# Attention and two gated FFNs on one core: a new plan for the weight chunks, and a new order of the quarter products

## The chip, the core and the metric

One core of a Trainium2 chip runs the whole program. The metric is device time in microseconds (us). TensorE (PE) multiplies, ScalarE (ACT), VectorE (DVE) and GpSimd (POOL) work on tiles, and SyncE (SP) issues nearly all DMAs. Each engine runs its own instructions in order and waits for the others by semaphores.

## The reference, cut to what matters

```python
scores = where(mask, q @ k.T / sqrt(D), -1e9)     # 4 batches, 8 heads, 576 x 64; heads 0-3 local, 4-7 strided
x = softmax(scores) @ v                            # as 2304 tokens x 512
xn = x / sqrt(mean(x * x) + 1e-6) * rms_g
y = (silu(xn @ w_gate) * (xn @ w_val)) @ w_out     # FFN 1, d_ff 1536
out = (silu(y @ w2_gate) * (y @ w2_val)) @ w2_out  # FFN 2, same sizes
```

All in float32. The kernel writes each operand of the FFNs as a sum of a rounded half (`xh`, `hh`, w[:, 0]) and its residual (`xl`, `hl`, w[:, 1]) and multiplies three of the four pairs.

## The kernel before

**Stages.** First the attention of batch 0; then its other batches are woven into the *early segments* of FFN 1: six segments of tokens (256 to 512 wide) times chunks 0 to 5 (a chunk is 128 of the 1536 hidden columns). From about 406 us on come five *passes* (chunks 6 to 8 and 9 to 11 of FFN 1, then 0 to 3, 4 to 7 and 8 to 11 of FFN 2), each over three *blocks* of 768 tokens.

**A chunk in a block.** Gate and value of a chunk are made from two halves of the 768 tokens by a scheme with seven *quarter products* instead of eight. A product is six matmuls of 128 x 384 (`Chunk.mult`). Products 1, 6, 7 and 4 add up in one PSUM bank (x), products 2, or 5 and 3, in another (y). Between them stand helpers: after 1 a *seed* (ACT copies x to y), after 6 and 7 a *keep* (ACT copies x to SBUF), after 2 a silu, which frees y; 5 opens y again, an `add` on DVE reads it, 3 adds to it, and after 4 and 3 a `join` (product, ACT cast to hh, DVE residual hl) ends the use of x and y. Two pairs of banks take turns, so a chunk's x is the bank of the chunk after next. `lower` multiplies by w_out (six matmuls) for one half of the tokens, `blank` the same for the other half of the block before, from the list `left`.

**Weights.** A chunk's words come as three loads of 0.5 MB into a ring of three buffers `raw` (five in the pool `st`, once the attention has ended), are put together by two ACT and two DVE instructions (`scale`: `raw`, `dh`), combined by four POOL subtractions (`sums`), and split into rounded half (ACT) and residual (DVE). Kind c keeps the result in SBUF; p *parks* it in DRAM (`pk`), r *recalls* it later; d does w_out. The text given to `plan` is the order of these. `weights()` is called at each *point* (one or two per product); it starts the next entry when its `ready` allows, and begins its operations `lag` points later, `pace["op"]` per point. A scheduler then puts each engine's instructions in order; `behind` ties a weight operation behind the last urgent one on its engine.

**Activations.** `load_x` fetches an early segment's input into `xraw`, in the same ring as `raw`. `stage_x` fetches the next block's 768 tokens into `xst`, `sum_x` and `split_q` (POOL, with ACT casts) make the next block's operands during this block.

Lines: `matmul` is L66; the weight operations are L227 and L235 (ACT), L239 and L244 (DVE), L326 (POOL sums), L358 (ACT cast), L362 (DVE residual), L370 and L371 (stores); L865 loads xraw, L892 casts hh in the early segments; in the passes L1210 is the keep, L1216 the seed, L1220 the add, L1224 the silu, L1230, L1234 and L1235 the join, L1314 the eviction, L1165 `sum_x`, L1182 the split.

Of the kernel before, what the change touches and what calls it, by code (L numbers as in the profile page):

```python
# [18 lines left out]
PRIO = 200  # L19
# [6 lines left out]
def attn_ffn_ffn(ctx: ExitStack, tc: tile.TileContext, q, k, v, w1g, w1v, w1o, rms_g, w2g, w2v, w2o, out):  # L26
# [178 lines left out]
    rack = {"pool": dec, "free": 3, "bufs": 3, "dh": 2}  # L205
    racks = [rack]
# [15 lines left out]
    def scale(cell, free=1):  # L222

        def high():
            cell["h"] = cell["bk"]["pool"].tile([128, 512], F32, tag="dh", name="dh", bufs=cell["bk"]["dh"])
            with behind("act"):
                nc.scalar.activation(out=cell["h"], in_=cell["hw"].bitcast(F32), func=AF.Copy, scale=2.0 ** -112)  # L227

        def low():
            cell["r"] = cell["lw"]  # L230
            if spare:
                spare.append(spare.pop(0))
                cell["r"] = pp.tile([128, 512], U32, tag=spare[-1], name="lws")
            with behind("act"):
                nc.scalar.activation(out=cell["r"], in_=cell["lw"], func=AF.Copy, scale=LOW)  # L235

        def sign():
            with behind("dve"):
                nc.vector.scalar_tensor_tensor(out=cell["r"], in0=cell["hw"], scalar=0x80000000, in1=cell["r"], op0=ALU.bitwise_and, op1=ALU.bitwise_or)  # L239

        def join():
            h = cell["h"].bitcast(U32)
            with behind("dve"):
                nc.vector.scalar_tensor_tensor(out=h, in0=h, scalar=3, in1=cell["r"], op0=ALU.logical_shift_left, op1=ALU.bitwise_or)  # L244
            cell["bk"]["free"] += free

        return [low, high, sign, join]
# [9 lines left out]
    def weight_step(m, c, z, park=False):  # L257
# [11 lines left out]
        def second():  # L269
            lo(cell["t"], cell["h"])  # L270
            wt[m, c, z] = cell["t"]
            wdone.add((m, c, z))
# [15 lines left out]
        def save():  # L288
# [4 lines left out]
            cell["bk"]["free"] += 1  # L293
# [3 lines left out]
                    lambda: (park or room[4]) and racks[0]["free"] >= 1, PRIO_W)  # L297
# [3 lines left out]
    def combined_step(m, c, how):  # L301
# [7 lines left out]
        def ready():  # L309
            if racks[0]["free"] < 2:  # L310
                return False
            return how == "park" or len(room[4]) >= n4 and len(room[2]) >= 7 - 2 * n4
# [7 lines left out]
        def sums():  # L320
# [4 lines left out]
            for z, a, b in ((0, b12, b11), (2, b22, b12), (1, b22, t[:, 0]), (3, b21, t[:, 1])):  # L325
                nc.gpsimd.tensor_tensor(out=t[:, z], in0=a, in1=b, op=ALU.subtract)  # L326
# [17 lines left out]
        def op(i, f):  # L344
            def g_():
                f(*parts[i])
                if i == len(parts) - 1 and f is (save if how == "park" else second):
                    g["bk"]["free"] += 1
                    if how == "park":
                        v["bk"]["free"] += 1  # L350
# [661 lines left out]
    plan("p19 p110 c16 d16 c17 c18 d17 d18 r19 d19 r110 d110 p111 p20 r111 d111 p21 r20 d20 r21 d21 p22 p23 r22 d22 r23 d23 "  # L1012
# [40 lines left out]
    def first_x():  # L1053
# [33 lines left out]
        for kk in range(2):  # L1087
            eager.extend((add("s1", "a21", "a22", ALU.add, kk), split(1, "a11", kk), split(4, "a22", kk), split(5, "s1", kk),
                          add("a21", "a11", "a21", ALU.subtract, kk), add("a11", "s1", "a11", ALU.subtract, kk), split(2, "a12", kk),
                          split(7, "a21", kk), add("a12", "a12", "a11", ALU.subtract, kk), split(6, "a11", kk), split(3, "a12", kk)))  # L1090
# [4 lines left out]
    for si, (m, t0, n, c0, c1) in enumerate(segs):  # L1095
# [11 lines left out]
        pace["op"] = 2.0  # L1107
        xs = xs_of.pop(si)
        state["tanh"] = True and att is not None
        for c in range(c0, c1):  # L1110
# [6 lines left out]
            if att and not steps and not active_att():  # L1117
# [6 lines left out]
                racks.insert(0, {"pool": pools["st"][0], "free": 5, "bufs": 5, "dh": 5})  # L1124
# [68 lines left out]
    class Chunk:  # L1193
# [44 lines left out]
        def step(self, i):  # L1238
# [104 lines left out]
    for n, (m, cs, t0) in enumerate(work):  # L1343
# [52 lines left out]
        state["lag"], state["wait"] = 10 if n else 5, 9  # L1396
        for z in (1, 0, 0, 2, 6, 0, 5, 7, 0):
            step(chunks[0], z) if z else blank()
            if z == 5 and nxt:
                cell = stage_x(nxt[0], nxt[2])  # L1400
            if z == 2:
                spare[:] = ya[halves[0].n:]
        for i, c in enumerate(chunks[:-1]):
            c1 = chunks[i + 1]
            step(c1, 1)
            step(c, 4)
            step(c, 3)
            if t0 + 2 * HN == NT:
                used((m, c.c, False))
            step(c1, 2)  # L1410
            if i == 0 and nxt:
                sum_x(cell)
            if i == k - 2:
                pace["op"] = 0.6 if n else 0.8
# [5 lines left out]
            if i == k - 2:  # L1420
                for j in J:
                    halves[0].fetch(j)
            while left:
                blank()
            lower(i, 0)
        c = chunks[-1]
        spare.clear()
        step(c, 4)
        step(c, 3)
        if t0 + 2 * HN == NT:  # L1430
            used((m, c.c, False))
        left = [piece(halves[1], c, g, other_done if g is G[-1] and c is chunks[-1] else None) for g in G for c in chunks]
        lower(k - 2, 1)
        blank()
        blank()
        for j in J:
            halves[1].fetch(j)
        lower(k - 1, 0)
        lower(k - 1, 1)
        blank()  # L1440
# [35 lines left out]
```

## Time and profile before

| | us |
|---|---|
| median of 3 runs (1057.32 to 1061.37) | 1059.54 |
| profiled execution | 1058.73 |
| its span | 1056.9 |
| PE busy | 992.2 (94%) |
| DVE, ACT, POOL busy | 589.0, 575.5, 472.9 |
| mean granted clock of PE | 0.964 |
| DMA | 181.60 MB, 172 GB/s |

PE is the busiest engine. In the page's 40 slices it is below 9 tenths in the first six (the attention), in the sixteenth and the twenty-second. A wait's row names the waiting instruction, the releaser and three numbers: us in total, times, longest. The granted clock is 1.00 at 2.4 GHz and 0.50 at 1.2 GHz.

### The profile page before, as it was taken

The numbers are of one execution on the slowest core, as the hardware profiler recorded it, in microseconds if no ns is written. First come the engines' busy times: TensorE is split into PE (matmuls) and PEld (weight loads), VectorE is DVE, ScalarE is ACT, GpSimd is POOL, SyncE is SP. The second block draws the span as 40 slices with busy tenths as digits, with TensorE's granted clock in tenths as the row PEclk, the third lists the DMA queues.
The fourth block names the chain that finished last, engine by engine and source line by source line (L and its number), as shares of the span: only waits on it lengthen the run. The fifth ranks groups of instructions, "written<-read, shape, count | busy, mean of one in ns | idle before, by whom it ended". The sixth has DMA issues, their size and how long they took to land. (4 is left out here: it accounts for less than half of the span.)

```text
span 1056.9 us, 16819 instructions
## 1 busy us (share of the span) xinstructions
PE 992.2 (94%) x5804; PEld 905.4 (86%) x5804; DVE 589.0 (56%) x1289; ACT 575.5 (54%) x1435; POOL 472.9 (45%) x485
## 2 busy tenths in 40 slices
PE   5758979999999997999987999999999999999998
PEld 4647869878778986999987999999998999899997
DVE  3779546445434186764756666555547665633433
ACT  5878745636633355753663565656547455643431
POOL 3312212203100294675956865837557473745500
PEclk9758989999999998999999999999999999999999
DMA  7576445224105129677687595257862739815021
GB/s 196 157 221 182 146 135 161 66 65 127 40 26 185 53 89 348 203 251 243 209 256 246 201 343 181 92 188 255 285 237 75 254 126 349 269 64 180 30 80 60
DMA packets 153277, 181.60 MB, mean 172 GB/s; under 512 B 44132, under 2 KB 120364, under 8 KB 153192
## 3 DMA queue, kind: packets, MB, share of 16 engines
q1 hardware_dynamic: 153000, 180.25, 52.6%
q8 instruction: 46, 0.75, 0.3%
q14 instruction: 39, 0.32, 0.1%
q0 software_dynamic: 192, 0.28, 0.1%
HBM read 123.60 MB, written 56.89 MB: 171 GB/s over the span
## 5 line engine op out<-in xcount | busy, mean ns | idle before, releaser
L1182 POOL TENSOR_TENSOR xl<-xst,xh 128x384 fp32r<-128x384 f32 x168 | 185.6, 1136 | 70.9 <-PE b_a L66 42.8
L66 PE MATMUL b_y<-xh,w 128*128 128x384 f32 x700 | 188.6, 336 | 4.0 <-ACT t L1210 4.0
L66 PE MATMUL b_g<-xh,w 128*128 128x384 f32 (+2 forms) x496 | 150.8, 352 | 9.7 <-ACT xh L905 7.0
L66 PEld LDWEIGHTS b_y<-xh,w 128*128 128x128 f32 x700 | 127.6, 188 | 7.6 <-ACT t L1210 5.7
L66 PE MATMUL b_a<-xh,w 128*128 128x384 f32 (+2 forms) x460 | 126.3, 338 | 5.6 <-DVE t L1220 5.5
L66 PE MATMUL b_v<-xh,w 128*128 128x384 f32 (+2 forms) x432 | 129.7, 350 | 0.0
L66 PE MATMUL b_y<-hh,w 128*128 128x256 f32 (+2 forms) x432 | 119.1, 347 | 3.7 <-ACT hh L892 3.7
L66 PE MATMUL b_y<-xl,w 128*128 128x384 f32 x350 | 117.4, 335 | 0.0
L66 PEld LDWEIGHTS b_g<-xh,w 128*128 128x128 f32 x496 | 93.3, 196 | 16.4 <-ACT xh L905 7.2
L66 PEld LDWEIGHTS b_a<-xh,w 128*128 128x128 f32 x460 | 83.9, 189 | 9.6 <-DVE t L1220 6.0
L635 POOL TENSOR_TENSOR e<-e,rc 128x384 f32<-128x384 f32 (+3 forms) x40 | 38.3, 961 | 119.6 <-DVE rc L629 84.3
L1181 ACT CAST xh<-xst 128x384 fp32r<-128x384 f32 x168 | 80.2, 522 | 12.5 <-POOL xst L1165 12.4
L66 PEld LDWEIGHTS b_y<-hh,w 128*128 128x128 f32 x432 | 78.3, 191 | 10.1 <-ACT hh L892 4.0
L66 PEld LDWEIGHTS b_v<-xh,w 128*128 128x128 f32 x432 | 79.7, 192 | 6.7 <-issue 0.4
L66 PE MATMUL b_g<-xl,w 128*128 128x384 f32 (+2 forms) x248 | 85.4, 344 | 0.0
L66 PE MATMUL b_a<-xl,w 128*128 128x384 f32 (+2 forms) x230 | 77.6, 337 | 0.0
L66 PE MATMUL b_y<-hl,w 128*128 128x256 f32 (+2 forms) x216 | 73.8, 342 | 2.4 <-DVE hl L893 1.7
L1165 POOL TENSOR_TENSOR s<-xst 128x384 f32<-128x384 f32 x28 | 28.8, 1049 | 104.5 <-DMA xst<-y_d 71.8
L66 PE MATMUL b_v<-xl,w 128*128 128x384 f32 (+2 forms) x216 | 73.5, 340 | 0.0
L66 PEld LDWEIGHTS b_y<-xl,w 128*128 128x128 f32 x350 | 65.7, 188 | 1.8
L66 PE MATMUL b_y<-w,hh 128*128 128x512 f32 x216 | 67.1, 392 | 0.0
L618 ACT ACTIVATE e<-e,nb 128x96 f32<-128x96 f32 (+2 forms) x152 | 56.6, 376 | 19.2 <-DVE nb L609 19.2
(210 smaller groups left out, 2198.3 us busy)
## 6 DMA issues: line engine op xcount, KB each, us to landing
w<-pk SPq DMA_DIRECT2D x39, 512.0 KB
pk<-raw SPq DMA_DIRECT2D x65, 256.0 KB
xst<-y_d SPq DMA_DIRECT2D x18, 768.0 KB
raw<-in_moe_w_gate_dram SPq DMA_DIRECT2D x24, 512.0 KB
raw<-in_moe_w_val_dram SPq DMA_DIRECT2D x24, 512.0 KB
raw<-in_moe_w_out_dram SPq DMA_DIRECT2D x24, 512.0 KB
part<-ob SPq DMA_DIRECT2D x48, 256.0 KB
ob<-part SPq DMA_DIRECT2D x36, 256.0 KB
```

The costliest lines, as they stand in the source:

```text
L66: traced(nc.tensor.matmul(out_, a, b_, start=start, stop=stop, **how))
L618: r = nc.scalar.activation(out=e[:qn, i, :kn], in_=e[:qn, i, :kn], func=AF.Exp, bias=nb[:qn, i:i + 1], scale=-1.0, accum_out=sums[:qn, i:i ...
L635: eng.tensor_tensor(out=e[:qn, :nt, :kn], in0=e[:qn, :nt, :kn], in1=rc[:qn, :nt].unsqueeze(2).to_broadcast([qn, nt, kn]), op=ALU.mult)
L1165: eng.tensor_tensor(out=out_[:, kk], in0=a[:, kk], in1=b[:, kk], op=op)
L1181: nc.scalar.copy(out=xh[:, kk], in_=src[:, kk])
L1182: eng.tensor_tensor(out=xl[:, kk], in0=src[:, kk], in1=xh[:, kk].bitcast(F32), op=ALU.subtract)
```

## The change

- **Plan.** Before, 13 chunks were parked (9, 10, 11 of FFN 1 and ten of FFN 2); now 11: chunk 6 of FFN 1 is parked and recalled, chunk 11 of FFN 1 and chunks 0 and 1 of FFN 2 are kept. A chunk is only parked once the attention has ended (`att is None`).
- **Counts.** A released buffer counts as free 6 points later; a second count (`words`) of buffers limits the first operation of a chunk, and rises 4 to 8 points after the last use.
- **Lags and paces** change (in the passes 12 points from load to first operation, where it was 9), POOL's sums get a higher priority, and product 6's split comes earlier in `first_x`.
- **Order of the products.** A chunk's products 7 and 5 now stand in the next cycle, and 6 before 2; x is staged after the first product of a block; the fetches of partial sums stand earlier.

```diff
-            fit = [st for st in begun if clock[0] - st.at >= st.lag]
+            fit = [st for st in begun if clock[0] - st.at >= st.lag and (not hasattr(st[0], "cell") or words(st[0].cell["bk"]) > 0)]
...
+    def back(bk, n):
+        bk["back"].append((clock[0] + 6, n))
...
+    def spent(bk, n):
+        bk["wback"].append(clock[0] + n)
+        bk["wback"].sort()
...
-            return how == "park" or len(room[4]) >= n4 and len(room[2]) >= 7 - 2 * n4
+            return how == "park" and att is None or how != "park" and len(room[4]) >= n4 and len(room[2]) >= 7 - 2 * n4
...
-            for z, a, b in ((0, b12, b11), (2, b22, b12), (1, b22, t[:, 0]), (3, b21, t[:, 1])):
-                nc.gpsimd.tensor_tensor(out=t[:, z], in0=a, in1=b, op=ALU.subtract)
+            with tc.high_priority(offset=PRIO):
+                for z, a, b in ((0, b12, b11), (2, b22, b12), (1, b22, t[:, 0]), (3, b21, t[:, 1])):
+                    nc.gpsimd.tensor_tensor(out=t[:, z], in0=a, in1=b, op=ALU.subtract)
...
-    plan("p19 p110 c16 d16 c17 c18 d17 d18 r19 d19 r110 d110 p111 p20 r111 d111 p21 r20 d20 r21 d21 p22 p23 r22 d22 r23 d23 "
+    plan("p16 p19 p110 r16 d16 c17 c18 d17 d18 p22 r19 d19 r110 d110 p23 c111 d111 c20 d20 c21 d21 r22 d22 r23 d23 "
...
-        pace["op"] = 2.0
+        pace["op"] = 2.5 if si < NA - 1 else 1.5
+        state["lag"], state["wait"] = (6, 6) if att is None else (3, 4)
...
                 self.mult(self.y, 5, True)
+                self.add(self.vb, self.vb)
             elif i == 7:
                 self.mult(self.x, 7, False)
                 self.vb = self.keep("t3", 2)
-                self.add(self.vb, self.vb)
...
-        state["lag"], state["wait"] = 10 if n else 5, 9
-        for z in (1, 0, 0, 2, 6, 0, 5, 7, 0):
-            step(chunks[0], z) if z else blank()
-            if z == 5 and nxt:
-                cell = stage_x(nxt[0], nxt[2])
...
+        state["lag"], state["wait"] = 10 if n else 8, 12
+        step(chunks[0], 1)
+        blank()
+        if nxt:
+            cell = stage_x(nxt[0], nxt[2])
+        blank()
+        spare[:] = ya[halves[0].n:]
+        step(chunks[0], 6)
+        if len(left) > 2:
+            blank()
+        step(chunks[0], 2)
         for i, c in enumerate(chunks[:-1]):
             c1 = chunks[i + 1]
             step(c1, 1)
+            step(c, 7)
+            step(c, 5)
+            blank()
+            lower(i - 1, 0)
             step(c, 4)
+            if i == k - 3 and nxt:
+                sum_x(cell)
+            step(c1, 6)
+            step(c1, 2)
             step(c, 3)
...
-            step(c1, 2)
-            if i == 0 and nxt:
-                sum_x(cell)
...
-            step(c1, 6)
-            blank()
-            lower(i - 1, 1)
-            step(c1, 5)
-            step(c1, 7)
...
             while left:
                 blank()
-            lower(i, 0)
+            lower(i - 1, 1)
```

SP's queue in the attention, about 85 to 120 us, before: `raw` are weight loads, `pk_9` the parking of chunk 9.

```order
L812 DMA x_d_1_994<-x_410 128x2x320
L218 DMA raw<-in_moe_w_out_dram 128x1024
L218 DMA raw<-in_moe_w_gate_dram 128x4x256
L218 DMA raw<-in_moe_w_val_dram 128x4x256
L218 DMA raw<-in_moe_w_gate_dram 128x4x256
L475 DMA qn_1292<-in_q_dram 108x1x320 x4
L477 DMA qn_1292<-in_q_dram 18x4x128
```

The same place now.

```order
L838 DMA x_d_1_961<-x_378 128x2x320
L237 DMA raw<-in_moe_w_out_dram 128x1024
L891 DMA xraw<-x_d_1_961 128x2x256 x2
L891 DMA xraw<-x_d_1_961 128x2x64 x2
L501 DMA qn_1246<-in_q_dram 108x1x320 x4
L503 DMA qn_1246<-in_q_dram 18x4x128
```

The three loads of chunks 9 and 10 have gone, and the loads of the second segment's input stand in their place.

ACT's queue at the end of the early segments, before: the last `sg` and `hh`, then the first seed of the passes (`b_v<-b_g`).

```order
L884 ACTIVATE sg<-b_a_4484 128x512
L235 ACTIVATE raw<-raw 128x512
L227 ACTIVATE dh<-raw 128x512
L358 CAST w_8_5_4482<-raw 128x512
L892 CAST hh<-sg 128x512
L251 CAST w_7_2_4548<-dh 128x512
L235 ACTIVATE raw<-raw 128x512
L358 CAST w_8_7_4483<-raw 128x512
L227 ACTIVATE dh<-raw 128x512
L251 CAST w_8_2_4574<-dh 128x512
L1216 COPY b_v<-b_g 128x384
```

The same place now; the first two `raw` and `dh` are chunk 8's gate, the second two its value, the third `raw` is w_out of chunk 7.

```order
L910 ACTIVATE sg<-b_a_4476 128x512
L255 ACTIVATE raw<-raw 128x512
L247 ACTIVATE dh<-raw 128x512
L918 CAST hh<-sg 128x512
L255 ACTIVATE raw<-raw 128x512
L247 ACTIVATE dh<-raw 128x512
L384 CAST w_8_1_4547<-dh 128x512
L1243 COPY b_v<-b_g 128x384
L384 CAST w_8_3_4548<-dh 128x256
L255 ACTIVATE raw<-raw 128x512
L76 COPY ob<-b_y_4331 128x512
L76 COPY ob<-b_y_4333 128x512
```

The load that ACT needs between `sg` and `hh` is another one, and chunk 8's work stands nearer to the passes.

ACT's queue in a cycle of a block of the first pass, before; each product leaves one row. `t_5482` and `t_5513` are the keeps of chunk 6's products 6 and 7, `t_5576` and `t_5591` those of chunk 7.

```order
L1210 COPY t_5482<-b_g 128x384
L1210 COPY t_5513<-b_g 128x384
L1216 COPY b_a_5523<-b_a_5516 128x384
L1224 ACTIVATE b_g<-b_g 128x384
L1234 CAST hh<-b_g 128x384
L1224 ACTIVATE t_5563<-b_a_5523 128x384
L1234 CAST hh<-b_v 128x384
L1210 COPY t_5576<-b_a_5516 128x384
L1210 COPY t_5591<-b_a_5516 128x384
L1216 COPY b_v<-b_g 128x384
```

The same cycle now; `t_5490` and `t_5519` are the keeps of chunk 6, `t_5564` and `t_5605` those of chunk 7.

```order
L1237 COPY t_5490<-b_g 128x384
L1251 ACTIVATE t_5499<-b_v 128x384
L1243 COPY b_a_5511<-b_a_5504 128x384
L384 CAST raw<-raw 128x512
L1237 COPY t_5519<-b_g 128x384
L1251 ACTIVATE b_g<-b_g 128x384
L1237 COPY t_5564<-b_a_5504 128x384
L1261 CAST hh<-b_g 128x384
L1251 ACTIVATE t_5572<-b_a_5511 128x384
L1261 CAST hh<-b_v 128x384
L1237 COPY t_5605<-b_a_5504 128x384
L1208 CAST xh<-xst 128x384 x2
```

The keep of product 7 has moved behind the next chunk's seed, and the silu after product 4 (`b_g<-b_g`) stands nearer to that bank's next use.

## Rows read from the trace of the kernel before

**Rows 1.** Busy us (and instructions) by stretch: PE, PEld, DVE, ACT, POOL; clock, DMA.

```profile
325.00:406.60 81.60, 81.60 (x464) 72.06 (x463) 42.77 (x59) 36.60 (x72) 37.79 (x33) 1.00 0.41 133
406.60:419.20 12.60, 7.25 (x19) 5.35 (x18) 9.36 (x13) 7.73 (x14) 5.32 (x6) 0.59 0.94 344
419.20:1056.90 637.70, 623.29 (x3339) 590.73 (x3338) 356.40 (x568) 334.60 (x726) 362.38 (x356) 0.99 0.58 196
```

**Rows 2.** What PE waited for: us in total, times, longest.

```profile
PE b_g L66 <- ACT xh L905: 7.0, 1, 7.0
PE b_a L66 <- DVE t L1220: 5.5, 1, 5.5
PE b_y L66 <- ACT t L1210: 4.0, 4, 2.9
PE b_y L66 <- ACT hh L892: 3.7, 1, 3.7
...
PE b_a L69 <- issue: 2.3, 1, 2.3
PE b_y L66 <- DVE hl L893: 1.7, 1, 1.7
```

**Rows 3.** Stretches right after PE's waits, columns as in rows 1.

```profile
122.10:125.40 3.30, 3.27 (x19) 2.81 (x20) 1.77 (x12) 2.30 (x11) 0.66 (x1) 0.51 0.53 180
138.90:142.60 3.70, 3.63 (x16) 3.43 (x17) 1.88 (x4) 1.32 (x4) 0.00 (x0) 0.50 0.84 304
413.10:419.20 6.10, 6.08 (x15) 5.01 (x16) 5.42 (x9) 3.75 (x7) 0.00 (x0) 0.51 0.98 371
580.90:586.30 5.40, 5.34 (x17) 5.35 (x18) 2.96 (x6) 2.51 (x6) 2.41 (x3) 0.50 0.26 97
...
536.40:540.00 3.60, 0.68 (x4) 0.36 (x3) 0.65 (x1) 1.03 (x2) 3.38 (x4) 1.00 0.68 181
```

**Rows 4.** Timeline of ACT in the attention: start, us, instruction, [idle before <-releaser].

```profile
120.12 0.62 ACT L358 CAST raw<-raw 128x512 fp32r<-128x512 f32 x1 [3.60 <-DMA pk<-raw]
...
138.51 0.71 ACT L905 CAST xh<-xraw 128x256 fp32r<-128x256 f32 x2 [3.92 <-DMA xraw<-x_d]
```

**Rows 5.** Timeline of SP's queue in the attention.

```profile
84.90 0.64 SPq L812 DMA_DIRECT2D x_d<-x  x1
...
134.07 0.38 SPq L865 DMA_DIRECT2D xraw<-x_d  x1
```

**Rows 6.** Timelines at the entry of the passes: ACT, then SP's queue.

```profile
408.35 0.67 ACT L235 ACTIVATE raw<-raw 128x512 uint32<-128x512 uint32 x1 [3.88 <-DMA raw<-in_moe_w_out_dram]
...
409.97 0.62 ACT L892 CAST hh<-sg 128x512 fp32r<-128x512 f32 x1
...
400.77 0.34 SPq L218 DMA_DIRECT2D raw<-in_moe_w_out_dram  x1
```

**Rows 7.** Timelines at the two longest waits in the passes: POOL, DVE, ACT.

```profile
576.32 1.94 POOL L1165 TENSOR_TENSOR s<-xst 128x384 f32<-128x384 f32 x2 [6.57 <-DMA xst<-x_d]
...
578.97 1.47 DVE L362 TENSOR_TENSOR dh<-dh,raw 128x512 fp32r<-128x512 f32 x1 [8.28 <-POOL raw L326]
...
538.66 0.67 ACT L227 ACTIVATE dh<-raw 128x512 f32<-128x512 f32 x1 [4.96 <-DMA pk<-dh]
```

**Rows 8.** Timelines of a fourth product and its join: PE, ACT, DVE.

```profile
565.92 0.33 PE L66 MATMUL b_g<-xh,w 128*128 128x384 f32 x1
...
566.96 0.33 PE L66 MATMUL b_v<-xh,w 128*128 128x384 f32 x1
...
567.16 0.47 ACT L1224 ACTIVATE b_g<-b_g 128x384 f32<-128x384 f32 x1 [0.58 <-PE b_g L66]
...
569.27 0.55 DVE L1235 TENSOR_TENSOR hl<-b_g,hh 128x384 fp32r<-128x384 f32 x1
```

**Rows 9.** Groups by shape: busy us, mean ns | idle before, what ended it.

```profile
L362 DVE TENSOR_TENSOR raw<-raw 128x512 fp32r<-128x512 f32 x26 | 22.2, 858 | 8.8 <-ACT raw L358 8.6
...
L1314 DVE TENSOR_TENSOR ob<-ob,b_y 128x384 f32<-128x384 f32 x24 | 12.7, 549 | 9.2 <-PE b_y L66 8.3 <-DMA raw<-in_moe_w_val_dram 0.9
```

More of the change, by code (lines that the diff above doesn't have):

```diff
@@ L203, in wait, with words, spaces @@
         pass
-    rack = {"pool": dec, "free": 3, "bufs": 3, "dh": 2}
-    racks = [rack]
+    racks = [{"pool": dec, "free": 3, "bufs": 3, "dh": 2, "back": [], "words": 2, "wback": []}]
+    def back(bk, n):
+        bk["back"].append((clock[0] + 6, n))
+    def words(bk):
+        while bk["wback"] and bk["wback"][0] <= clock[0]:
+            bk["words"] += 1
+            bk["wback"].pop(0)
+        return bk["words"]
+    def spent(bk, n):
+        bk["wback"].append(clock[0] + n)
+        bk["wback"].sort()
+    def spaces():
+        bk = racks[0]
+        while bk["back"] and bk["back"][0][0] <= clock[0]:
+            bk["free"] += bk["back"].pop(0)[1]
+        return bk["free"]
     parked = {}
@@ L244, in join @@
                 nc.vector.scalar_tensor_tensor(out=h, in0=h, scalar=3, in1=cell["r"], op0=ALU.logical_shift_left, op1=ALU.bitwise_or)
-            cell["bk"]["free"] += free
+            back(cell["bk"], free)
+        high.cell = cell
         return [low, high, sign, join]
@@ L270, in second @@
             lo(cell["t"], cell["h"])
+            spent(cell["bk"], 4)
             wt[m, c, z] = cell["t"]
@@ L292, in save @@
             nc.sync.dma_start(out=d[:, 1], in_=a)
-            cell["bk"]["free"] += 1
+            back(cell["bk"], 1)
+            spent(cell["bk"], 6)
             parked[m, c, z] = d
         return Step([load] + scale(cell, int(not park)) + ([high, low, save] if park else [first, second]),
-                    lambda: (park or room[4]) and racks[0]["free"] >= 1, PRIO_W)
+                    lambda: (park or room[4]) and spaces() >= 1, PRIO_W)
     QUARTERS = ((1, 2), (5, 6), (7, 4), (3,))
@@ L346, in g_ @@
                 f(*parts[i])
+                if f is (save if how == "park" else second) and parts[i][0][0] in (1, 3):
+                    spent((g if parts[i][0][0] == 1 else v)["bk"], 6 if how == "park" else 8)
                 if i == len(parts) - 1 and f is (save if how == "park" else second):
-                    g["bk"]["free"] += 1
+                    back(g["bk"], 1)
                     if how == "park":
-                        v["bk"]["free"] += 1
+                        back(v["bk"], 1)
                     else:
@@ L1123, in attn_ffn_ffn @@
                 open_pool("st", "st", 0, bufs=1)
-                racks.insert(0, {"pool": pools["st"][0], "free": 5, "bufs": 5, "dh": 5})
+                racks.insert(0, {"pool": pools["st"][0], "free": 5, "bufs": 5, "dh": 5, "back": [], "words": 5, "wback": []})
                 room[4] += [(pools["wpb"][0], f"v{i}") for i in range(2)]
@@ L1409, in attn_ffn_ffn @@
                 used((m, c.c, False))
[L1410 to L1422 removed]
             while left:
                 blank()
[L1425 removed]
+            lower(i - 1, 1)
         c = chunks[-1]
         spare.clear()
+        for j in J:
+            halves[0].fetch(j)
+        for j in J[:3]:
+            halves[1].fetch(j)
+        step(c, 7)
+        step(c, 5)
+        lower(k - 2, 0)
         step(c, 4)
@@ L1431, in attn_ffn_ffn @@
             used((m, c.c, False))
+        lower(k - 2, 1)
         left = [piece(halves[1], c, g, other_done if g is G[-1] and c is chunks[-1] else None) for g in G for c in chunks]
[L1433 to L1437, printed above, removed]
+        for _ in range(3):
+            blank()
         lower(k - 1, 0)
         lower(k - 1, 1)
-        blank()
+        for j in J[3:]:
+            halves[1].fetch(j)
         while due:
```

9 lines of the change are left out of this document (4 added, 5 removed).

## The prediction

> **What bounds the kernel now.** I read three views in order: the busy times by stretch, the list of what TensorE (PE) waited for, and the timelines of the engines it waited for, at the four places where it stood longest. The profiled execution took 1058.73 us, its span is 1056.9 us, and 1.8 us lie around it. The median of the three runs is 1059.54 us, 0.8 us above; I work against 1058.7 and add nothing for that.
>
> PE is busy 623.3 of the 637.7 us from 419 us on, and all of the 81.6 us before the passes [rows 1]. The matmuls are the same in both kernels, so a change can give back only PE's idle time and the time in which PE ran at the lower clock. From 119 us on PE's idle time is nearly all in six rows [rows 2]: 2.3 and 7.0 us in the attention, 3.7 and 1.7 us at the entry of the passes, 5.5 and 4.0 us inside them. Four of these waits are followed by a stretch at a granted clock of 0.50 or 0.51, the 1.2 GHz level, with PE busy for 3.27, 3.63, 6.08 and 5.34 us in it [rows 3]; half of that comes back if the wait goes. So the most that is there is:
> attention 2.3 + 7.0 + (3.27 + 3.63) / 2 = 12.8 us;
> entry 3.7 + 1.7 + 6.08 / 2 = 8.4 us;
> passes 5.5 + 4.0 + 5.34 / 2 = 12.2 us; together 33.4 us.
> The waits of the first 119 us I leave out: PE's order in after is the same there, and SP's up to 94 us.
>
> The clock has a row against a rule. After the 2.9 us wait at 536 us the stretch still shows 1.00, the 2.4 GHz level [rows 3]. The Trainium skill, TensorE: Matmul & The Clock Gate, section "HAM oscillation — how this bites in real kernels", says that waits on DMA between bursts of matmuls let the clock fall, so that the next burst starts slow. By that rule this wait is paid twice as well, and some 1.6 us more (half of the shortest slow stretch above) would come back. The trace agrees at four places and not at this one; my sum goes by the row.
>
> **The attention: 12 us back.** ACT stood 3.60 us at 120.12 for the store of a parked chunk (a residual written over a buffer that is still being stored), and hh and the copy that frees a PSUM bank stood behind it in ACT's queue [rows 4]. That ends in PE's 2.3 us. At 138.51 ACT waited 3.92 us for xraw, the second segment's input, which PE had waited for since 131.7 us [rows 4]. Its data were in DRAM from the store at 84.90 on, but the load was issued at 134.07 only [rows 5]: xraw takes its buffers from the ring of three that the weight chunks use, and the parked chunks 9 and 10 held them. In the new order of SP the xraw loads stand where those chunks' loads stood, with no parking beside the attention (the condition "att is None"). Nothing is late behind them that I can find: PE's order there is unchanged, and DVE, ACT and POOL only lose work. From below: the next link, the attention's own chain of softmax steps, may show up to 2 us; from above all 12.8. I take 12.
>
> **The parking moves to 325 to 406 us: nothing, with cover.** Three chunks (6, 9, 10) are parked there now, and chunk 6 comes back from DRAM instead of being built in place: two more chunks of work than before in that stretch. A chunk is eight instructions on DVE, 0.86 us for one of the two-input ones [rows 9], so some 7 us, two of them 14 us; ACT's and POOL's share is less. DVE is busy 42.8 of 81.6 us there, ACT 36.6 and POOL 37.8 [rows 1], so DVE goes to 57 of 82 and still fits. What hides it is that a gate chain has two chunks of slack there (`waiting` holds two). If that cover fails, the price is a wait like the one at the entry, 4 to 5 us. Below zero it can hardly go, since PE has no idle time in that stretch. I take 0 and keep 5 for the range.
>
> **The entry: 5 of 8.4 us back.** ACT waited 3.88 us for a w_out load that SP had issued at 400.77, and the hh cast of the last early chunk, ready long before, ran at 409.97 behind it [rows 6]. In the new order the two ACT instructions between the last sg and its hh read a gate matrix whose load stands before the three recalls and the x loads on SP, so hh should run when its data are there. Two other loads can hold ACT now. Right behind hh stand two instructions on chunk 8's value matrix, whose buffer chunk 7 frees late, and behind them the seed of chunk 6, for which PE has two blanks and a product, 3.8 us. And the w_out load still stands behind three recalls (0.5 MB each) and 1.6 MB of x, with the DMA engines full (0.94, 344 GB/s [rows 1]): 3.1 MB take 9 us; behind it stands the keep of product 6, with some 3 us to spare. So between all (8.4 back) and the same waits moved (0 back); I take 5, nearer to the first because the waiter with no slack is gone.
>
> **The passes: 11 of 12.2 us back.** At 576.32 POOL had stood 6.57 us for the next x, with a weight sum (L326) queued behind, DVE stood 8.28 us for that sum at 578.97, and the add that PE needs (L1220) was behind it; at 536 us ACT stood 4.96 us for a store at L227, and the keep (L1210) was behind that [rows 7]. The change acts on each: x is staged about five products earlier (after the first product, not after the fifth), summed in pass 1 after six products and two or three blanks instead of five products and one, and loads get 12 steps before their first use where there were 9; a released buffer counts as free only after 4 to 8 steps. It also moves PE: between a seed and the product that needs it stood 2 products, now 4 and a down product; between 5 and 3 stood 7, a down product, 1 and 4, now a down product, 4, 6 and 2, with the add one ACT hop earlier. A product is 1.04 us (565.92 to 566.96 [rows 8]), so most late helpers get 1 to 2 us more before PE notices. Two parked chunks fewer also take 2 × 3.6 MB out of the 181.6 MB. Against it: staging earlier makes SP wait longer for POOL's last splits, with weight loads behind it. Ends: 0 and 12.2; I take 11, since the two long waits have named causes that the order removes.
>
> **New waits: 2 us.** Two distances get shorter. From the fourth product of a chunk to the first product of the chunk after next, which overwrites its bank, there were six products and more; now three, 3.1 us, in the first cycle of a pass, and 4.2 in later ones. The chain in between (silu, product, cast, residual) ran from 566.96 to 569.82, 2.9 us [rows 8], with little in its way; one foreign DVE instruction of 0.86 us in a link makes PE wait 0.6 us in a first cycle (6 such in the passes of three chunks). And the next block's first product now comes 9 matmuls (1.6 us) after the last write to the bank it takes, where it was 15; the eviction takes 0.55 us [rows 9], or 1.4 behind one foreign instruction: hidden but for a few tenths. 6 × 0.3 us makes 2 us; from 0 to 8 for the range (14 boundaries at 0.3 and 6 cycles at 0.6).
>
> **Sum:** 12 + 0 + 5 + 11 − 2 = 26 us off 1058.7, 1033 us.
>
> **Rivals.**
> 1. Only the attention gains. The DMA engines stay full at the entry and whenever x, recalls and weights meet, and ACT or POOL waits for some other load. For it: the full DMA engines at the entry, and waits of this kind at three different operations, so that any order may have its own. Against it: bigger lags and fewer bytes. It gives 1058.7 − 12 to 1058.7 − 12 + 2: 1047 to 1049 us.
> 2. The attention does not gain: xraw still comes late, behind chunk 5's buffers in the same ring, or the softmax chain takes the place. Against it: those three loads stood before 94 us. It gives 1058.7 − 16 + 2 = 1045 us.
> 3. All six waits go and no new ones come: 1058.7 − 33.4 = 1025 us.
> 4. Slower: the chain from the fourth product to the bank's next use is longer than its new distance in every cycle, since weight work stands in its links. There are 6 × 2 + 9 × 3 = 39 cycles. At 0.72 us each it eats the 28 us gained; at 1.0 us it gives 1058.7 − 28 + 39 = 1070 us. For it: a chain of 2.9 us against 3.1. Against it: 33 of the 39 cycles have 0.7 to 1 us of down products more, and the chain would need two foreign instructions each time.
>
> **How the numbers follow.** Forecast 0.56 (own range 1026 to 1041), rival 1 0.20, rival 2 0.06, rival 3 0.10, rival 4 0.08. About 0.5% (5.3 us) is what a measurement of this kernel can tell from no change, so faster means below 1054. Faster: 0.56 + 0.10 + 0.06 + 0.15 = 0.87, where a quarter of rival 1 ends closer because the parking's 5 us or more new waits come on top; the same: 0.05 + 0.02 = 0.07; slower: 0.06 of rival 4. The range from 1022 to 1050 takes in rivals 1 to 3 and leaves out most of rival 4.
>
> **What would show it.** In the trace after: xraw loads soon after 94 us and no wait of PE for xh near 130 us, with the clock at 1.00 there; at the entry no PE wait for hh, and ACT perhaps waiting for a w_out load; POOL not waiting over 2 us for xst with L350 (the sum) behind it. Wrong would be: PE waiting for a first product's bank in many cycles (rival 4: PE waits on hl or on ACT's copies), or waits of over 2 us for loads inside the passes (rival 1).

## The result, and the profile after

The changed kernel takes 1066.8 us (median of 6 runs, 1064.2 to 1073.0), the kernel before 1059.7 us (6 runs): a ratio of 1.008, 95% interval 1.0052 to 1.0109. The forecast was 1033 us, with a range of 1022 to 1050: wrong in size and in sign.

The profiled execution has a span of 1067.7 us, 10.8 us more than before. Both kernels compute the same things, so I matched the casts to hh, in ACT's order, between the two traces. First the timeline of ACT in the kernel after, at five of them (the 3rd, 7th and 36th early ones, and the 12th and 36th in the passes):

```profile
110.81 0.39 ACT L918 CAST hh<-sg 128x256 fp32r<-128x256 f32 x1
...
138.64 0.41 ACT L918 CAST hh<-sg 128x256 fp32r<-128x256 f32 x1 [0.59 <-DVE sg L915]
...
403.44 0.62 ACT L918 CAST hh<-sg 128x512 fp32r<-128x512 f32 x1 [0.79 <-DVE sg L917]
...
480.76 0.48 ACT L1261 CAST hh<-b_y 128x384 fp32r<-128x384 f32 x1 [0.26 <-DVE b_y L1257]
...
629.60 0.48 ACT L1261 CAST hh<-b_y 128x384 fp32r<-128x384 f32 x1 [0.24 <-DVE b_y L1257]
```

The same casts in before, from the same view, and what each stretch gained or lost (difference of two neighbouring lags):

| stretch ends at | before, us | after, us | lag | lost (+) or won (-) in it |
|---|---|---|---|---|
| 3rd early cast | 102.99 | 110.81 | +7.8 | +7.8 |
| 7th | 144.10 | 138.64 | -5.5 | -13.3 |
| 36th (entry, [rows 6]) | 409.97 | 403.44 | -6.5 | -1.1 |
| 12th of the passes | 478.96 | 480.76 | +1.8 | +8.3 |
| 36th of the passes | 628.82 | 629.60 | +0.8 | -1.0 |
| end of the span | 1056.9 | 1067.7 | +10.8 | +10.0 |

The attention's gain is there and as large as forecast. It is spent three times: before it, in the 77 us after the last early cast, and in the last 438 us.

The attention. ACT's cast of xraw and SP's issue of the load in after, then a window (columns as in [rows 1]): the load stands at 102.87 us where it stood at 134.07 [rows 5], ACT waits 0.71 us for it where it waited 3.92 [rows 4], and PE is busy throughout at a clock of 1.00 where before had stood 7.0 us:

```profile
105.58 0.71 ACT L931 CAST xh<-xraw 128x256 fp32r<-128x256 f32 x2 [0.71 <-DMA xraw<-x_d]
...
102.87 8.62 SPq L891 DMA_DIRECT2D xraw<-x_d  x4
...
120.00:145.00 25.00, 25.00 (x252) 23.41 (x249) 9.61 (x48) 15.14 (x55) 3.45 (x5) 1.00 0.17 58
```

The loss ahead of it. The same window of after, then of before. The matmuls are the same ones in the same order. PE is busy all the time in after, but the granted clock stays at 0.50, the 1.2 GHz level, where before shows 0.95 (and the experiment e16 below 1.00):

```profile
84.00:96.00 12.00, 12.00 (x51) 10.70 (x52) 6.32 (x33) 6.70 (x29) 1.03 (x1) 0.50 0.72 224
```
```profile
84.00:96.00 12.00, 9.20 (x69) 8.29 (x70) 10.19 (x57) 11.44 (x49) 6.24 (x5) 0.95 0.62 201
```

The passes. Windows of after by stage, to be held against [rows 1], and the last stretch of before. From the 36th cast of the passes on, the same work takes 438.1 us where it took 428.1. PE stands 11.4 us in it where it stood 5.3; most of the rest is clock, two stretches of 3.4 us at 0.50, behind waits of 1.98 us (at 824.5) and 1.69 us (at 909.7), which cost half their length:

```profile
319.00:401.40 82.40, 82.10 (x465) 72.20 (x464) 47.88 (x68) 41.08 (x82) 40.96 (x38) 1.00 0.69 231
...
629.60:1067.70 438.10, 426.75 (x2207) 394.53 (x2206) 227.53 (x368) 216.73 (x470) 216.84 (x216) 0.99 0.47 165
```
```profile
629.00:1056.90 427.90, 422.64 (x2205) 391.91 (x2203) 226.94 (x367) 215.53 (x468) 219.70 (x219) 1.00 0.51 172
```

What PE waited for in after from 403 us on (us in total, times, longest). The long waits of [rows 2] (xh, the add t, the keep t) are gone or shorter. In their place stand many waits of 1 to 2.3 us for hh and hl (the two halves that a down product needs) and for ob, an eviction that frees a bank:

```profile
PE b_g L66 <- ACT hh L1261: 4.4, 4, 1.7
PE b_y L66 <- ACT hh L1261: 4.3, 4, 1.9
PE b_g L66 <- DVE ob L1341: 3.4, 2, 2.0
PE b_g L66 <- ACT t L1237: 3.1, 2, 2.3
PE b_y L66 <- DVE hl L1262: 2.8, 3, 1.4
PE b_y L66 <- DVE ob L1341: 2.3, 1, 2.3
PE b_y L66 <- ACT hh L918: 2.3, 1, 2.3
```

### The profile page after: what moved, and what is told of

It is laid out like the page before. It is cut to its first block, busy times and chain, and to the rows that moved or that the text cites. A ratio compares the mean times of both kernels' runs of the same rounds, so it can differ in the third digit from the quotient of the medians.

```text
span 1067.7 us, 16823 instructions
## 1 busy us (share of the span) xinstructions
PE 999.8 (94%) x5804; PEld 907.5 (85%) x5804; DVE 583.8 (55%) x1289; ACT 575.1 (54%) x1435; POOL 469.8 (44%) x485
## 4 chain that ended last, share of the span: by engine, by line
PE 64%; DMA 9%; POOL 8%; DVE 7%; ACT 4%; issue 4%; SPq 2%; DVEq 0%; POOLq 0%; ACTq 0%
PE b_y L66 25%; PE b_a L66 15%; PE b_g L66 12%; PE b_v L66 10%; DMA raw<-in_moe_w_gate_dram 3%; PE b_a L69 2%; POOL xl L1209 2%; POOL raw L350 2%; POOL xl L1107 1%; POOL xst L1192 1%; DMA y_d<-ob 1%; SPq L501 1%; DMA xraw<-x_d 1%; DVE raw L388 1%; ACT raw L255 1%
## 5 line engine op out<-in xcount | busy, mean ns | idle before, releaser
L1209 POOL TENSOR_TENSOR xl<-xst,xh 128x384 fp32r<-128x384 f32 x168 | 181.2, 1102 | 120.0 <-ACT xh L1208 120.0
L66 PE MATMUL b_y<-xh,w 128*128 128x384 f32 x700 | 190.9, 339 | 5.6 <-DVE ob L1341 2.3
L66 PEld LDWEIGHTS b_y<-xh,w 128*128 128x128 f32 x700 | 129.0, 190 | 10.9 <-DVE ob L1341 3.1
L1208 ACT CAST xh<-xst 128x384 fp32r<-128x384 f32 x168 | 77.7, 516 | 11.2 <-POOL xst L1192 11.0
```

Source lines behind the costliest of these rows:

```text
L66: traced(nc.tensor.matmul(out_, a, b_, start=start, stop=stop, **how))
L1208: nc.scalar.copy(out=xh[:, kk], in_=src[:, kk])
L1209: eng.tensor_tensor(out=xl[:, kk], in0=src[:, kk], in1=xh[:, kk].bitcast(F32), op=ALU.subtract)
```

## The experiments

Ratios are to the kernel before, run beside each experiment on the same chip. Its median was between 1059.7 and 1062.7 us, so kernels that ran at different times are compared by their ratios; 0.001 is 1.06 us, and brackets hold the 95% interval.

**The attention alone (e1, e5).** Before, with parking only after the attention and the new list of chunks; e1 has the new pace of steps too.

```
-return how == "park" or len(room[4]) >= n4 ...
+return how == "park" and att is None or how != "park" and len(room[4]) >= n4 ...
-plan("p19 p110 c16 d16 c17 c18 ...
+plan("p16 p19 p110 r16 d16 c17 c18 ...
 e1 also: pace["op"] = 2.5 if si < NA - 1 else 1.5; lag, wait = (6, 6) or (3, 4)
```

> The kernel before, with only the part that concerns the attention and the parking: the new list of chunks, parking only while no attention runs, and the pace of the stretch from the attention to the passes. Counts of buffers, sums, loads and the order of the passes are those of before. After against before, matched instruction by instruction, lost 7.5 us up to 104 us, won 13 us from there to 145 us, and won about 2 us at the entry. Theory A (the 13 us belong to the plan, the 7.5 us to the clock, which stood at 0.50 from 80 to 97 us by the chance of that run): 13 us off, about 1047 us. Rival (the 7.5 us belong to this part too): 1052 to 1054 us. Rival that the 13 us need the late counts too: 1060 us.

> The experiment with the attention's part alone, without its pace: only the new list of chunks and parking only while no attention runs; the steps' pace from the attention to the passes is that of before. With the pace, the attention won 13.8 us, but PE lost 17.1 us from the entry (395 us) to 477 us where before loses 5.6: at 405.88 us PE had waited 6.16 us for the seed behind a w_out load that was 8.4 us on its way. Theory D (the faster steps put the loads, recalls and fetches of the entry into one heap): about 8 us off, 1047 us. Rival E (the list itself does, chunk 6 comes back as a recall beside x and w_out): no change, 1054 to 1056 us.

e1 took 1055.5 us, 0.9943 (0.9910 to 0.9977); e5 1055.5, 0.9936 (0.9908 to 0.9964). So this part wins 6 us, not 13, and the pace has no share: theory D is out. In e1's profile the 7th early cast comes 12.9 us earlier than in before (131.2 against 144.1 us) and the first 103 us cost nothing. The rest is given back at the entry, and the chain that does it starts some 40 us earlier. e1's ACT, then SP's queue, ACT and PE at the entry:

```profile
361.04 0.62 ACT L358 CAST raw<-raw 128x512 fp32r<-128x512 f32 x1 [7.06 <-DMA pk<-raw]
...
365.68 3.00 ACT L1080 CAST xh<-xst 128x384 fp32r<-128x384 f32 x7 [0.17 <-DMA part<-ob]
...
394.37 1.92 SPq L1160 DMA_DIRECT2D xst<-x_d  x3
396.33 0.62 SPq L218 DMA_DIRECT2D raw<-in_moe_w_out_dram  x1
...
404.79 0.66 ACT L235 ACTIVATE raw<-raw 128x512 uint32<-128x512 uint32 x1 [5.68 <-DMA raw<-in_moe_w_out_dram]
...
405.88 0.69 PE L66 MATMUL b_v<-xh,w 128*128 128x384 f32 x1 [6.16 <-ACT b_v L1217]
```

ACT waits 7.06 us for the store of a parked chunk, and casts of the first block's x (L1080) stand behind it. POOL's splits (L1081) need these casts; the last split ends at 394.34 us. SP stands 8.0 us for it before the next x loads, and the w_out load is queued behind them. That load is 8.4 us on its way, beside 1.5 MB of x and the fetches of parts. ACT waits for it, the seed (L1217) is queued behind, and PE waits for the seed.

**Chunk 6 built in place (e11, e16, e12).** The list has `c16 d16` again, and no `p16`, `r16`: no store and no recall of that chunk.

```
-plan("p16 p19 p110 r16 d16 c17 c18 d17 d18 p22 ...
+plan("p19 p110 c16 d16 c17 c18 d17 d18 p22 ...
```

> The kernel before with parking only after the attention, its pace, and the new list of chunks with chunk 6 built in place; without late counts of buffers and without priority for the sums. Theory (the attention's wait and the recall at the entry are all that matters): 1055.5 - 10 = 1045 us. Rival (the late counts, which keep a released buffer from being counted at once, are needed for it): 1050 to 1055 us.

> The kernel with the old order and the short lead (1053.7 us), with chunk 6 built in place as before has it and not parked and fetched back, which takes 0.5 MB of stores and 0.5 MB of recall out of the stretch up to the entry. From the entry to 475 us PE lost 14.6 us there against 5.6 in before. Theory K (the recalls beside x, w_out and the fetches of parts make the entry's waits): 3 to 6 us off, 1048 to 1051 us. Rival (any list that parks after the attention has this heap; the weights of chunks 7 and 8 come later still): no change or slower, 1054 to 1058 us.

> The kernel after with chunk 6 built in place as in before, and nothing else changed. Theory K (the recall of chunk 6 beside x, w_out and the parts makes the entry's waits; with the old order it cost 10 us): 1066.8 - 10 = 1057 us, and PE's excess from the entry to 480 us falls from 14 us to 4 to 8. Rival L (the entry of the new order has other waits, for keeps and evictions, and they stay): 1064 to 1067 us.

e16 (on e1) took 1045.0 us, 0.9848 (0.9804 to 0.9893), against 0.9943; e11 (on e8, below) 1043.5, 0.9858 (0.9815 to 0.9901), against 0.9938. By the ratios that is 10 and 8 us, and parking chunk 6 cost, with the old order, most of what the attention had won. e16 has neither the late counts of buffers nor the priority of the sums, so they are not needed for it. Windows around the entry in e1 and e16 (columns as before): PE is busy 5.7 us more in e16.

```profile
384.00:420.00 36.00, 26.38 (x112) 22.57 (x111) 21.18 (x29) 16.57 (x33) 17.47 (x17) 0.86 0.78 258
```
```profile
384.00:420.00 36.00, 32.12 (x154) 29.40 (x154) 24.84 (x38) 21.49 (x42) 14.59 (x16) 0.91 0.86 294
```

Theory K puts the cost down to the recall in a full DMA queue at the entry. The rows show another way. SP's queue in e16, then ACT in after:

```profile
383.83 1.91 SPq L1160 DMA_DIRECT2D xst<-x_d  x3
385.78 1.92 SPq L397 DMA_DIRECT2D w<-pk  x3
389.89 0.33 SPq L218 DMA_DIRECT2D raw<-in_moe_w_out_dram  x1
```
```profile
368.16 0.62 ACT L384 CAST raw<-raw 128x512 fp32r<-128x512 f32 x1 [6.04 <-DMA pk<-raw]
```

In e16, w_out has three recalls and the x loads just ahead of it and is 8.0 us on its way, much as in e1; but POOL's last split ends at 381.91, SP does not stand for it, and w_out is issued 6.4 us earlier. ACT's wait for a store, of 5.5 to 7.1 us between 360 and 369 us, is in all eleven kernels with chunk 6 parked and in none of the seven others. The edit takes out the stores and the recall together, so the share of each is not shown.

e12, the same edit on the kernel after, gave 1067.1 us, 1.0039 (1.0009 to 1.0069): 4 us by the ratio, with overlapping intervals, and not 10. With the new order the rest comes back as other waits: in e12 PE waits 20.3 us for hh and hl from the entry on, in after 14.0. By the median that is L. Counted from the 7th early cast to the 12th of the passes, against before, the chunk costs 8.7 us in e1 (10.8 lost against 2.1 in e16), 7.1 in e8 (9.0 against 1.9 in e11), and 1.9 in after (7.3 against 5.4 in e12).

**The order of the passes (e3, e2).** e3 is before with the new order alone, e2 is after with the old order. (Both edits also touch the pace of weight operations at the end of the first block, 0.8 in the old order.)

> The kernel before, with only the new order of the passes (products, lower products, blanks, staging and sum of x, fetches, the add, and the splits). Theory B (order): 18 us slower than before, or 10 if the two long waits of before (8 us) go: 1068 to 1078 us. Rival C (weight work): the order by itself costs nothing, 1050 to 1060 us.

> The kernel after, with the order of the passes put back to that of before (products, lower products, blanks, staging and sum of x, fetches, the add, and the splits), all the rest as after. Theory B (order): the 18 us that PE lost more than before from 425 us on (36.2 us of excess against 18.0) are waits that the new order makes, for hh behind ACT's casts, for evictions and for keeps: 1066.8 - 18 = 1049 us, less if the two long waits of before come back. Rival C (weight work: late counts, priority of the sums, loads 12 steps ahead put weight instructions in front of casts and evictions): the waits stay, about 1066 us.

e3 took 1079.0 us, 1.0152 (1.0101 to 1.0203): the order alone costs 16 us. By the same casts as above, e3's profiled execution loses 10.8 us against before from the 36th early cast to the 12th of the passes, 0.9 from there to the 36th, and 8.8 in the last stretch. e2 took 1063.5, 1.0041 (1.0009 to 1.0072), only 4 us better than after, with overlapping intervals: beside the order there is a second cost, as rival C said. First the order. Where does it wait? After, at the end of a block, DVE, ACT and PE:

```profile
905.73 0.56 DVE L1247 TENSOR_TENSOR b_y<-t,b_y 128x384 f32<-128x384 f32 x1
906.20 0.68 DVE L264 SCALAR_TENSOR_TENSOR dh<-dh,lws 128x512 uint32<-128x512 uint32 x1
906.79 0.56 DVE L1257 TENSOR_TENSOR b_y<-b_y,t 128x384 f32<-128x384 f32 x1
...
907.04 0.48 ACT L1237 COPY t<-b_y 128x384 f32<-128x384 f32 x1 [1.07 <-PE b_y L66]
907.42 1.34 ACT L1208 CAST xh<-xst 128x384 fp32r<-128x384 f32 x3
908.66 0.66 ACT L255 ACTIVATE raw<-raw 128x512 uint32<-128x512 uint32 x1
909.22 0.47 ACT L1261 CAST hh<-b_y 128x384 fp32r<-128x384 f32 x1
...
909.74 0.50 PE L66 MATMUL b_g<-w,hh 128*128 128x512 f32 x1 [1.69 <-ACT hh L1261]
```

Product 3 ended near 905.2; the add, a weight operation and the join on DVE end at 907.35; then five instructions of ACT stand in front of hh. PE has only a short down product, 7 and 5 to do meanwhile (905.1 to 908.05), and waits 1.69 us.

**Two distances put back (e6, e7, e14, e10).** In after the down product of the last but one chunk stands two products behind its product 3, where before had four; and the next block's first product stands 9 matmuls behind the last write to its bank, where before had 15 (6 and 12 in the passes of FFN 2).

```
 e6:  step(c, 5)                     e7:  -for _ in range(3):
     -lower(k - 2, 0)                     +for _ in range(2):
      step(c, 4)                               blank()
     +lower(k - 2, 0)                      lower(k - 1, 0); lower(k - 1, 1)
      step(c, 3)                          +blank()
 e14: e3 with both    e10: after with both, and loads 9 steps ahead, lag 5
```

> The kernel after with one exchange: in the last chunk of a block product 4 goes ahead of the down product of the chunk before it (first half), which so stands three products behind the product 3 that its hh comes from, where after has two. Theory F (this distance, 2.8 us against a chain of add, product, cast and residual with weight work in front, makes PE's waits for hh at 432, 585, 809 and 907 us, 7.0 us in all): 4 to 6 us off, 1061 to 1063 us. Rival C (the waits are made by weight work and only move to the next link): no change, 1067 us.

> The kernel after with one of the three blanks of a block's end put back behind its last down product, where before had one, so that the next block's first product comes some 15 matmuls after the last write to its bank and not 9. Theory G (this distance makes PE's waits for an eviction at 444, 558 and 822 us, 5.8 us in all): 3 to 5 us off, 1062 to 1064 us. Rival: it takes a blank from the products ahead and only moves the waits, 1067 us or slower.

> The kernel before with the new order of the passes (1079.0 us), with two of its distances put back: the down product at a block's end one product later, and one blank behind the last down product. Theory F/G (these two distances make most of what the new order costs): 8 to 14 us off, 1065 to 1071 us. Rival (the whole of the new cycle is tighter, and waits move to other links): 1075 to 1079 us.

> The kernel after with three things mended: loads 9 steps ahead and lag 5, the down product of a block's end one product later, and one blank back behind the last down product. If the three costs add (about 9 for the lead, 3 for each of the others, from the medians 1063.5 to 1053.7, and 1066.8 to 1064.3): 1052 to 1055 us, level with the old order at the same lead (1053.7). If the new order has still another cost: 1058 to 1062 us.

e6 took 1064.3 us, 1.0030 (1.0000 to 1.0061); e7 1066.4, 1.0026 (0.9994 to 1.0058); e14 1072.5, 1.0108 (1.0061 to 1.0156), 5 us under e3; e10 1063.8, 1.0026 (1.0000 to 1.0052). By the ratios e6 and e7 are 5 to 6 us under after each, about as expected, though the intervals overlap. e14 gets back 5 of the order's 16 us, not 8 to 14, and e10 gets no further than e6 or e7 alone, where 1052 to 1055 us was expected: the costs do not add up over the whole kernel. What each edit took away is seen in the last stretch, where little else happens: what PE waited for there, first in e6, then in e7, then in e10.

```profile
PE b_g L66 <- DVE ob L1341: 2.7, 3, 1.2
PE b_y L66 <- DVE ob L78: 1.3, 1, 1.3
...
PE b_g L66 <- ACT hh L1261: 0.5, 2, 0.2
```
```profile
PE b_g L66 <- ACT hh L1261: 3.4, 2, 1.7
PE b_y L66 <- DVE hl L1262: 1.4, 2, 1.0
```
```profile
PE b_y L66 <- DVE hl L1262: 0.8, 1, 0.8
PE b_y L66 <- ACT hh L1261: 0.7, 3, 0.2
...
```

Summed from this view, from the 36th cast of the passes to the end, and how much longer than in before this stretch is by the casts (us):

| | hh and hl | ob | all | longer by |
|---|---|---|---|---|
| old order (before, e1, e2, e5, e8, e11, e13, e15, e16) | 0.2 to 0.7 | 0 to 0.3 | 0.9 to 4.5 | -1.4 to 3.0 |
| new order (after, e3, e4, e9, e12) | 4.7 to 6.5 | 1.0 to 3.5 | 7.3 to 8.5 | 8.4 to 10.0 |
| e6: down product later | 0.5 | 4.0 | 5.9 | 6.3 |
| e7: blank back | 5.1 | 0 | 6.4 | 7.1 |
| e10: both; e14: both | 1.5; 2.3 | 0; 0 | 1.9; 3.1 | 2.2; 4.7 |

Each edit alone removes its own kind of wait and leaves the other, and both together remove most of both, on after as on e3. That settles F and G for this stretch: the two distances make 7 to 8 of its 9 to 10 us in after and e9, and about half of its 9 us in e3. What stands in front of the eviction in after, DVE and PE at the start of another block:

```profile
819.45 1.55 DVE L388 TENSOR_TENSOR w<-raw,w 128x512 fp32r<-128x512 f32 x1
820.92 1.51 DVE L276 TENSOR_TENSOR w<-dh,w 128x512 fp32r<-128x512 f32 x1
822.36 1.47 DVE L388 TENSOR_TENSOR w<-raw,w 128x512 fp32r<-128x512 f32 x1
...
824.49 0.44 PE L66 MATMUL b_g<-xh,w 128*128 128x384 f32 x1 [1.98 <-DVE ob L1341]
```

Three weight residuals of some 1.5 us each, while POOL is busy. From the entry to the 36th cast the two edits bring less, since waits move: e6 has 12.5 us of waits for ACT's keeps (t) from the entry on, after 3.3.

**Loads 12 or 9 steps ahead, and the sums (e8, e9, e4).** e8 is e2 with the loads 9 steps ahead and lag 5; e9 is after with the same; e4 is after with the sums on POOL at their old priority.

```
 e8, e9: -state["lag"], state["wait"] = 10 if n else 8, 12
         +state["lag"], state["wait"] = 10 if n else 5, 9
 e4:     -with tc.high_priority(offset=PRIO):   (around the four sums)
```

> The kernel after with the old order of the passes (1063.5 us, 8 us slower than the attention's part alone), and the loads of the passes 9 steps ahead of their first operation and not 12, with the old lag of 5. Theory H (loads that start 12 steps ahead keep the raw buffers and the DMA queues full): 1056 us, as the attention's part alone. Rival I (the late counts of buffers or the sums' priority cost it): 1063 us.

> The kernel after with the loads of the passes 9 steps ahead and lag 5 (the order of the passes stays new). With the old order this took 1063.5 to 1053.7 us. Theory H2 (the lead costs some 9 us in either order): 1057 us. Theory J (with the new order the waits are those for hh and evictions, which the lead does not make): 1064 to 1067 us.

> The kernel after, with the weight sums on POOL at their old priority. In the trace of after ACT or DVE stood behind a sum at 412 to 415 us, 442 to 444 and 581 to 583 us, each followed by a wait of PE of 1.9 to 2.4 us, and by half clock. Theory C1 (the priority makes these): about 8 us off, 1059 us. Theory B (the order makes the waits, whatever stands in front): no change, 1066 us, within 3.

e8 took 1053.7 us, 0.9938 (0.9907 to 0.9969): 11 us better than e2 by the ratio, theory H. It still has the late counts and the sums' priority, which e1 (0.9943) lacks, so with the old order these two cost nothing, and rival I falls. e9 took 1073.8, 1.0149 (1.0095 to 1.0202): 7 us worse than after, against both theories. e4 took 1067.5, 1.0060 (1.0028 to 1.0091): 2 us under after, within the noise: the sums' priority is not it, C1 falls. So a long lead costs 11 us in the one order and wins 7 in the other, and the order costs 22 us at the short lead (e9 against e8) and 4 at the long one (after against e2). Most of e9's loss is one place, DVE, POOL and PE there:

```profile
473.39 8.77 DVE L388 TENSOR_TENSOR dh<-dh 128x256 fp32r<-128x256 f32 x1
482.09 1.00 DVE L1341 TENSOR_TENSOR ob<-ob,b_y 128x384 f32<-128x384 f32 x2
...
474.49 0.73 POOL L350 TENSOR_TENSOR raw<-dh,raw 128x256 f32<-128x256 f32 x1
475.18 1.95 POOL L1192 TENSOR_TENSOR xst<-xst 128x384 f32<-128x384 f32 x2
477.10 1.93 POOL L1209 TENSOR_TENSOR xl<-s,xh 128x384 fp32r<-128x384 f32 x2
479.00 2.88 POOL L1209 TENSOR_TENSOR xl<-xst,xh 128x384 fp32r<-128x384 f32 x3
...
484.81 0.69 PE L66 MATMUL b_g<-xh,w 128*128 128x384 f32 x1 [8.30 <-DVE ob L1341]
```

A weight residual whose median is 0.43 us took 8.77 us and ended (482.16) just after POOL's run of work did (481.88); the evictions stood behind it, and PE 8.30 us behind them. Such a thing depends on how the engines' queues happen to meet, so e9's 7 us look to belong to this pairing of order and lead and to be no price of a step. Where e8's 11 us come from was not traced.

**Early staging of x (e13, e15).** The old order with x staged after the first product; e13 on e8, e15 on e11.

```
-if z == 5 and nxt:
+if z == 1 and nxt:
     cell = stage_x(nxt[0], nxt[2])
```

> The kernel with the old order and the short lead (1053.7 us), with one part of the new order: the next block's x is staged after a block's first product and not after its fifth. Theory M (early staging holds SP, whose weight loads then come late; it is a part of the new order's 20 us): 3 to 8 us slower, 1057 to 1062 us. Rival N (the prediction's: it lets POOL and DVE run earlier and takes waits away, 0 to 5 us faster): 1049 to 1054 us.

> The fastest version so far (old order, short lead, chunk 6 built in place, 1043.5 us), with x staged after a block's first product. Staging alone moved 1053.7 to 1052.3 us. If the two are independent: 1041 to 1044 us. If the entry now has no slack for x in front of the weight loads: 1046 to 1050 us.

e13 took 1052.3 us, 0.9913 (0.9885 to 0.9942), e15 1042.9, 0.9804 (0.9767 to 0.9840); both intervals overlap those of the kernels without it. With the old order, staging early neither costs nor wins what can be measured. e15 has the lowest median of all versions, 2% under before; e11's and e16's intervals overlap its own.

## Why the prediction was wrong, step by step

- **Attention, 12 us back: right.** 13.3 us in the profile, 12.9 in e1, for the reason given.
- **Parking at nothing: the first step that failed.** I asked only whether the engines had time for the extra work, and there the cover held: PE was busy 82.10 of 82.40 us from 319 us on. What I left out is that ACT waits for a parked chunk's store. I had read such a wait at 120.12 us [rows 4] and booked its end as a gain of the attention; it went along with the parking (6.04 us at 368.16 in after, 7.06 at 361.04 in e1) and, in e1, came out as PE's wait at the entry. The parked chunk 6 costs 8 to 10 us with the old order (e11 against e8, e16 against e1), about 4 in after (e12, not clear of noise). I had 5 us for it in the range and nothing in the sum.
- **Entry, 5 us back: wrong.** From the 36th early cast to the 12th of the passes after loses 8.3 us; PE waits there for 10.9 us where it waited 5.4 in before. The last early hh does run when its data are there (0.79 us for DVE), as I said, but PE still waits 2.30 us for it at 404.1 and 2.28 for a keep at 416.7. The other large waits, 1.69 us at 434.3, 2.35 at 446.5 and 1.44 at 463.3, are for hh, an eviction and hl, the kinds that the new order brings. In e1 the seed was the waiter, which I had named and given 3.8 us.
- **Passes, 11 us back: wrong.** The two long waits did go, but 1.0 us is all that the stretch around them won, and in e9 the same edits went with a wait of 8.30 us. That they were coincidences of one arrangement, and not the property of a step that the order could remove, is the reading that fits; it was not tested. Early staging, half of my argument, measures as nothing with the old order.
- **New waits, 2 us: the main failure.** The new order alone costs 16 us (e3). I looked for the distance that became shorter, and took the one from product 4 to the bank's next use (five products before, not six; three now); it hardly appears in PE's list. Two others account for most of the last stretch's loss in after and were in the order as well. One is from product 3 to the down product at a block's end, which I did not check: five instructions of ACT stood in front of hh there. The other is from the last down product to the next block, which I priced at a few tenths, with one foreign instruction of 0.86 us allowed in front: three of some 1.5 us stood there.
- **Rival 4** had the sign and, at 1070 us, nearly the time, but by another link.
- **The first 103 us**, left out of the sum because the order is unchanged, lost 7.8 us in the profiled execution through the clock.
- **The clock after 536 us.** The last row of [rows 3], from 536.40 us, is mostly the wait itself, with PE busy 0.68 of 3.60 us. The stretch behind it bears out what was read from it:

```profile
540.00:545.00 5.00, 5.00 (x30) 4.89 (x30) 4.26 (x9) 4.01 (x10) 1.25 (x2) 1.00 0.92 308
```

Open: the part of the order's 16 us that e14 does not get back, most of it before the 36th cast of the passes (the order's other parts, such as the earlier fetches of partial sums and the place of the add, were not tried alone); how much of the entry's 8.3 us in after is chunk 6 and how much the order, since removing one brings up the other's waits; why the order costs 22 us at one lead and 4 at the other beyond the one place shown; and what sets the clock's early stretch.

## What to carry to other kernels

When an order is changed, list for every product what it waits for and count the products between, before and after, at block ends too; compare each distance with the chain plus what may stand in front in the queues of ACT and DVE, here three to five instructions and not one. When work is moved, move its waits along in the estimate: a store that made ACT wait in the old place makes it wait in the new one, and what stands behind it there has to be followed to PE. One-off waits of 5 us in a profile can be coincidences: do not book them as gains unless the edit removes their cause in every cycle.

## What the runs showed of the hardware

Work on DVE with all operands in SBUF is stretched while POOL works. In e9 the 128x512 operations of L388 took 0.69 us on average with POOL idle (21 of them) and 1.26 with POOL busy for nine tenths of the time or more (26). The longest row stands in this group of L388 (ns, shortest, median, longest):

```profile
L388 DVE TENSOR_TENSOR dh<-dh x11: 415/426/8773, 335.4 to 920.6; 128x256 fp32r<-128x256 f32 x11
```

The Trainium skill, SBUF — State Buffer, section "SBUF: two separate sides", says that DVE and GpSimd share a pair of ports as an exclusive lock, held for a whole instruction, and that the other blocks. The trace agrees, and goes beyond one instruction: the row of 8.77 us spans eight of POOL's in a row. That the ports held it is read from the two ends; no run tried it alone. Rows of 3.9 to 4.6 us over four or five of POOL's stand in six other executions. DVE's 128x384 operations with an operand in PSUM took 0.56 us on average in e9, with POOL busy in the same sense (198 of them) or idle (143).

The clock can stay low while PE is busy: in after 17 us at 0.50 with PE busy all the time (80 to 97 us). 6 of the 18 profiled executions had 0.50 from 84 to 96 us with PE busy 12.0 us; 11 others had 0.89 to 1.00 there, and one 0.72. By the 3rd early cast the six had lost 5.4 to 8.3 us against before, the eleven -0.6 to 1.5. Five of the six are kernels with the new order, which does not touch this stretch, but four others with it are not among them; what decides it stays open. Nor does a wait's length alone tell whether the clock falls: in after the wait of 1.69 us at 909.7 was followed by a stretch at 0.50, those of 1.69 us at 434.3 and 811.8 by 1.00.
